# Two 64-column halves for the last key tile of the product with V, and other places for the products of a pair

## The chip, the cores and the metric

The kernel runs on one NeuronCore of a Trainium2 chip. The metric is the device time of one execution in microseconds, the median of several runs; smaller is better. Beside it there is one profiled execution, from which all durations below come.

## What is computed

Attention over 4 batches, 8 heads, 576 positions and 64 elements per head, with a bias from a small network over the distance of two positions, and behind it a mixture of experts: every token takes one of 8 experts (a local gate may keep the expert of the token before), goes through its two layers and is scaled by the gate's probability.

```python
scores = scale * np.matmul(q, k.transpose(0, 1, 3, 2))
...
scores = scores + bias.transpose(2, 0, 1)[None, :, :, :]
scores = scores - np.max(scores, axis=-1, keepdims=True)
attn = np.exp(scores)
attn = attn / (np.sum(attn, axis=-1, keepdims=True) + 1e-09)
return np.matmul(attn, v).astype(np.float32)
...
h = np.maximum(x[b, s] @ w1[e], 0.0)
out[b, s] = p[e] * (h @ w2[e])
```

## The kernel before

**Pairs and units.** Attention goes by pairs `(p, b)`: two heads x = 0, 1 of batch b, 16 pairs in all. The 576 queries of a pair are five tiles, in the order `QORD` = 1, 2, 0, 3, 4; a full tile is two units, one for each head, and the last tile, of 64 queries, is one unit for both. A pair is thus nine units, numbered u. The first four pairs (p = 0) run interleaved, while the bias is still being made; the other twelve run one after the other.

**One unit.** `emit_s` multiplies q with k in fp16 (L305, L306; L316 for the last tile) into one of two PSUM tiles `sps`. VectorE adds the bias and takes the row's extreme (L325), ScalarE takes the exponential with the row sum (L330). `emit_t` transposes the result on TensorE (L396, the last keys in L412, for the last tile L410), and ScalarE and VectorE copy it into the tile `eT` (L402, L400, L413).

**Product with V.** `emit_av(p, b, g)` multiplies `eT` with V in fp32 for a group of query tiles: g = 0 holds tiles 1 and 2 (256 columns), g = 1 tiles 0, 3 and 4 (320 columns). The output is a PSUM tile `av` with head 0 in partitions 0 to 63 and head 1 in 64 to 127; there is one such tile. Keys 512 to 575 of both heads make up a common tile j = 4, V being laid out with zeros so that a single product over 128 columns serves both (L422). For j = 0 to 3 each head has a product of 64 columns (L426). In group 1 a small product (L434) folds the two row sums of the last query tile into columns 320 and 321. VectorE copies `av` to `xt` (L440) and the sums to `sums` (L442).

For eight pairs (`DMP`, the first eight behind p = 0) group 0 goes another way: the probabilities are split into two fp16 parts (L336, L346), SP's queue transposes them by DMA (L350), and `av_split` multiplies them in three parts n = 0, 1, 2 (L363 for the last keys, L369 in 64-column halves, 8 for each part), with a copy to `xt` (L380).

Behind group 1, `emit_recip` inverts the sums, `emit_gates` multiplies `xt` with the gate weights (L534 for p = 2 and 3, into a free part of the same PSUM tile), and `emit_rows` transposes `xt` back (L454, L456), scales it (L466, L471), splits it in two fp16 parts and stores it through SP, five units later for the eight split pairs.

**The order.** Every step is entered with a key, its unit plus an offset, and the steps are issued in the order of the keys. SP's queue keeps that order from the first to the ninth pair behind p = 0; on the other engines a planner may still pass over a step that isn't ready and issue a later one. S of unit u has the key u, the DMA steps and stores u + 0.1, other steps u + 0.4, transposes u + `LTS`, the parts of `av_split` u + `LA0` (u is the last unit of tile 2), `emit_av` of group 0 u + `LAN`, and counted from the unit of the last tile, `emit_av` of group 1 u + `LA1`, gates u + `LL`, rows u + `LOUT`. The pairs with p = 0 have offsets of their own (`LB0`, `LC0`, `LO0`), which stay. Counted from the first unit of a pair, u is 3 for tile 2 and 8 for the last tile. The last pair's products stand in a part written out by hand.

Of the kernel before, what the change touches and what calls it, by code (L numbers as in the profile page):

```python
# [49 lines left out]
def build(tc, nc, io):  # L50
# [6 lines left out]
    def load_pack(name, fields):  # L57
        t = const.tile(list(io[name].shape), F32, name="c_" + name)
        nc.sync.dma_start(out=t, in_=io[name])
        views, o = [], 0  # L60
        for w in fields:
            views.append(t[:, o:o + w])
            o += w
        return views
# [38 lines left out]
    ident, wgl, c8e, s0m, tokv, c128, iota, emadd, amat, gmat, edif, fold, hmask, bcut = load_pack("cpb", CPB)  # L103
# [158 lines left out]
    e_t, eT_t, hs_t = {}, {}, {}  # L262
# [153 lines left out]
    def emit_av(p, b, g, part=None):  # L416
        n = (256, 320)[g]
        if part != 1:
            av_t[p, b] = av_ps.tile([128, 512], F32, name="av")
        av, eT, vt = av_t[p, b], eT_t[p, b, g], v_t[b, p]  # L420
        if part != 1:
            nc.tensor.matmul(out=av[:, 0:n], lhsT=vt[:, 4], rhs=eT[:, 8, 0:n], start=True, stop=False)  # L422
        js = (0, 1, 2, 3) if part is None else (0, 1) if part == 0 else (2, 3)
        for j in js:
            for x in range(2):
                nc.tensor.matmul(  # L426
                    out=av[64 * x:64 * x + 64, 0:n], lhsT=vt[:, j, 64 * x:64 * x + 64],
                    rhs=eT[:, 2 * j + x, 0:n], start=False, stop=(j == 3),
                )
        if part == 0:  # L430
            return
        eT_t.pop((p, b, g))
        if g == 1:
            nc.tensor.matmul(out=av[0:64, 320:322], lhsT=fold, rhs=hs_t.pop((p, b)), start=True, stop=True)  # L434
        if g == 0:
            xt_t[p, b] = xt_p.tile([128, SP], F32, name="xt")
            if p >= NP - 2:
                nc.vector.memset(xt_t[p, b][:, S:SP], 0.0)
        xt = xt_t[p, b]
        nc.vector.tensor_copy(out=xt[:, 256 * g:256 * g + n], in_=av[:, 0:n])  # L440
        if g == 1:
            nc.vector.tensor_copy(out=sums[0:64, p, 4, b], in_=av[0:64, 320:322])  # L442
# [107 lines left out]
    def rtile(shape, name, dt=F32):  # L550
        return rbox["p"].tile(shape, dt, name=name)
# [83 lines left out]

    bias_step(12)
    LB0, LC0, LO0 = 3.2, 6, 1.28
    LTS = (3.2, 3.2, 2.95, 3.2, 3.95)
    LA0, LAN, LA1, LL, LOUT = (5.8, 8.55, 8.8), 10.62, (6.35, 6.6), 8.6, 8.72
    NU = len(units)  # L640
    ex_t = {}

# [427 lines left out]
    def pair_av1(p, b, part):  # L1070
        emit_av(p, b, 1, part)
        if part != 0:
            emit_recip(p, b)
# [3 lines left out]
    def at(key, f, *a):  # L1077
        ev.append((key, len(ev), partial(f, *a)))

    for u in range(NU):  # L1080
        gi, hh = units[u]
        p, b, qt = groups[gi]
        at(u, unit_s, u)
        at(u + 0.1, unit_r, u)
        at(u + (LB0 if p == 0 else LTS[QORD.index(qt)]), emit_t, u)
        at(u + 0.4, unit_x, u)
        if qt == QORD[1] and hh == 1:
            if (p, b) in DMP:
                for n in range(3):
                    at(u + LA0[n], av_split, p, b, n)  # L1090
            elif p:
                at(u + LAN, emit_av, p, b, 0)
            else:
                at(u + LC0 + 0.6, emit_av, p, b, 0)
        if qt == 4:
            if p:
                if LA1[0] == LA1[1]:
                    at(u + LA1[0], pair_av1, p, b, None)
                else:
                    at(u + LA1[0], pair_av1, p, b, 0)  # L1100
                    at(u + LA1[1], pair_av1, p, b, 1)
                at(u + LL, pair_gates, p, b)
                at(u + LOUT, pair_out, (p, b, gi))
            else:
                at(u + LC0 + 0.6, pair_av1, p, b, None)
                at(u + LC0 + LO0 - 0.01, pair_gates, p, b)
                at(u + LC0 + LO0, pair_out, (p, b, gi))
# [57 lines left out]
    out = io["out"]  # L1165
# [12 lines left out]
    oa, at = rtile([128, NG2, NB], "oa", F16), rtile([128, NG2, NB], "at", F16)  # L1178
# [63 lines left out]
    with fin:  # L1242
# [16 lines left out]
        for i in range(2):  # L1259
            nc.tensor.matmul(  # L1260
                out=cn[:, i:i + 1], lhsT=amat16[:, i], rhs=R["cs"][:, S - 1:S], start=True, stop=True
            )
        nc.vector.tensor_scalar(
            out=nbc.rearrange("p a k -> p (a k)"), in0=bcut[0:32], scalar1=cn[:, 0:1], scalar2=None, op0=ALU.is_lt
# [7 lines left out]
        for i in (2, 3):  # L1272
            nc.tensor.matmul(out=cn[:, 2 + i:3 + i], lhsT=amat[:, i], rhs=nb[:, 2:3], start=True, stop=True)
        nc.vector.scalar_tensor_tensor(
            out=R["thh"], in0=nb[:, 1:2], scalar=128.0, in1=cn[:, 1:2], op0=ALU.mult, op1=ALU.subtract
        )
        nc.vector.scalar_tensor_tensor(
            out=gp[:, 1], in0=cn[:, 1:2].to_broadcast([32, B]), scalar=-1.0, in1=gmat, op0=ALU.add, op1=ALU.mult
# [5 lines left out]
            out=rbox["h16"][:, 0:S], in0=R["cs"], scalar=R["thh"], in1=es, op0=ALU.is_gt, op1=ALU.mult  # L1284
# [3 lines left out]
            out=ecm[:, K1:NF], in0=c128[0:8, 0:NF - K1], scalar1=cn[0:8, 3:4], scalar2=None, op0=ALU.is_ge  # L1288
        )
        nc.vector.tensor_scalar(  # L1290
            out=ecm[:, NF:], in0=c128[0:8, 0:NH], scalar1=cn[0:8, 5:6], scalar2=None, op0=ALU.is_ge
        )
        nc.vector.tensor_scalar(
            out=hsh, in0=cn[:, 4:5], scalar1=cn[:, 3:4], scalar2=128.0 * (NF - K1), op0=ALU.subtract, op1=ALU.add
# [10 lines left out]
            out=ez, in0=ecm.unsqueeze(2).to_broadcast([8, NBLK, NE]),  # L1305
# [14 lines left out]
        for b in range(K1, K1 + 2):  # L1320
# [4 lines left out]
            out=mkp.rearrange("p k e -> p (k e)"), lhsT=on[0:8, 0:128], rhs=ez.rearrange("p k e -> p (k e)"),  # L1325
            start=True, stop=True,
        )
        for b in range(K1, K1 + 2):
# [6 lines left out]
            out=mk, in0=mkp, in1=emadd.unsqueeze(1).to_broadcast([128, NBLK, NE]), op=ALU.add  # L1335
# [19 lines left out]
        for i, m in enumerate((FSURE, HSURE)):  # L1355
            nc.vector.tensor_scalar(
                out=rest[:, i:i + 1], in0=emp[:, NBLK + i:NBLK + i + 1], scalar1=-float(m), scalar2=0.0,
# [5 lines left out]
            out=i1, in0=sls, scalar1=0.0, scalar2=float(NT // 2 - 1), op0=ALU.is_lt, op1=ALU.add  # L1363
# [5 lines left out]
            out=odh, in0=i1[:, NF:NF + HSURE], scalar1=2.0, scalar2=hmask[:, 1:2], op0=ALU.mult, op1=ALU.add  # L1369
# [155 lines left out]
```

## Time and profile before

| | us |
|---|---|
| median of 3 runs | 581.85 |
| lowest and highest | 580.81 and 583.0 |
| profiled execution, device time | 579.53 |
| its span in the profile | 577.7 |

The span goes from the first to the last instruction of the profiled execution; the device time holds about 1.8 us more around it. Engines are named PE (TensorE's matmuls), PEld (its weight loads), DVE (VectorE), ACT (ScalarE), POOL (GpSimd) and SP (the DMA queue). A number like L426 is a line of the kernel before.

### The profile page before, as it was taken

To read this page: it belongs to the slowest core of one execution; us is meant where nothing else is said; L and a number is where in the kernel's file an instruction comes from. 1 tells how busy PE (TensorE), PEld (TensorE's weight loads), DVE (VectorE), ACT (ScalarE), POOL (GpSimd) and SP (SyncE) were. 2 spreads that over 40 slices of the span, in tenths; PEclk is the share of its full clock that TensorE was granted. 3 is DMA by queue.
4 is the path that set the end of the run, shared out by engine and by line. 5 is a ranking of instruction groups with operands and counts; after the bars stand their busy time and mean duration, and the time that the engine had idled before them with its cause. 6 is when DMAs were issued, how large, how long until landed. Compare 5 with 4: busy or idle time off the path is not lost. (4 is left out here: it accounts for less than half of the span.)

```text
span 577.7 us, 14240 instructions
## 1 busy us (share of the span) xinstructions
PE 530.2 (92%) x5302; PEld 359.0 (62%) x5319; DVE 468.2 (81%) x914; ACT 436.6 (76%) x742; POOL 260.4 (45%) x293
## 2 busy tenths in 40 slices
PE   5679999989978999999899999999999999999991
PEld 1124445756755667767586676577686867777851
DVE  6888885688888989797888468779999799898950
ACT  5879877867978887877589865468998787986840
POOL 5200000795299969858547560622433354334111
PEclk9799999999999999999999998799999999999997
DMA  8766546756798799646084012866999947878240
GB/s 278 258 175 186 143 133 194 262 161 154 193 240 226 204 255 247 188 105 190 23 289 117 2 42 71 218 220 218 290 260 293 332 146 191 161 214 225 36 180 30
DMA packets 99613, 106.15 MB, mean 184 GB/s; under 512 B 66893, under 2 KB 76239, under 8 KB 95442
## 3 DMA queue, kind: packets, MB, share of 16 engines
q1 hardware_dynamic: 94752, 89.45, 55.0%
q0 software_dynamic: 4640, 15.43, 9.1%
q8 instruction: 44, 0.72, 0.5%
q10 hardware_dynamic: 146, 0.30, 0.2%
q14 instruction: 31, 0.25, 0.1%
HBM read 128.92 MB, written 20.80 MB: 259 GB/s over the span
## 5 line engine op out<-in xcount | busy, mean ns | idle before, releaser
L330 ACT ACTIVATE e<-e,st 128x576 f32<-128x576 f32 x144 | 111.5, 776 | 16.5 <-DVE st L325 13.1
L325 DVE CUSTOM_DVE_ANT_0 e<-sps,wb 128x576 f32<-128x576 f32 x144 | 107.0, 749 | 18.1 <-PE sps L306 13.3
L917 DVE TENSOR_TENSOR w<-wb,w 128x2048 bf16<-128x2048 f32 (+1 forms) x36 | 72.3, 2050 | 1.9 <-ACT w L910 1.6
L402 ACT COPY eT<-ta 128x512 f32<-128x512 f32 x96 | 55.0, 582 | 21.8 <-PE ta L396 14.6
L305 PE MATMUL sps<-kh,qs 128*128 128x288 f16 x256 | 68.3, 288 | 3.4 <-DVE st L325 2.8
L1014 POOL DMA_INDIRECT out_dram<-y,odx x17 | 30.3, 1781 | 90.2 <-ACT y L1004 58.9
L396 PE MATMUL ta<-c_cpb,e 128*128 128x128 f32 x448 | 70.1, 277 | 0.2
L306 PE MATMUL sps<-kl,qs 128*128 128x288 f16 x256 | 68.0, 286 | 0.0
L910 ACT CAST w<-wb 128x2048 f16<-128x2048 f32 (+1 forms) x40 | 63.8, 1641 | 2.6 <-DMA wb<-in_w_dram 2.6
L988 PE MATMUL yp<-w,hhT 128*128 128x512 f16 (+1 forms) x255 | 64.3, 384 | 1.5 <-ACT w L910 0.5
L211 PE MATMUL sps<-hd,c_cpa 128*32 128x512 f32 (+17 forms) x352 | 49.2, 517 | 15.0 <-DVE hd L197 10.6
L949 PEld LDWEIGHTS <-we 128*128 128x128 f16 (+1 forms) x1056 | 59.9, 98 | 2.4
L949 PE MATMUL sps<-xT,we 128*128 128x128 f16 (+1 forms) x1056 | 61.1, 219 | 0.0
L426 PE MATMUL av<-eT,vt 128*64 128x320 f32 (+1 forms) x384 | 60.8, 424 | 0.0
L396 PEld LDWEIGHTS ta<-c_cpb,e 128*128 128x128 f32 x448 | 52.0, 141 | 10.0 <-issue 2.2
L197 DVE TENSOR_SCALAR hd<-tab,bp 128x448 f32<-128x448 f32 (+17 forms) x130 | 50.1, 445 | 3.6 <-PE sps L211 3.6
L949 PE MATMUL sps<-xT,wb 128*128 128x128 f16 (+3 forms) x1056 | 50.1, 209 | 0.7 <-issue 0.7
L949 PEld LDWEIGHTS <-wb 128*128 128x128 f16 (+1 forms) x1056 | 48.1, 99 | 3.8 <-issue 2.5
L917 DVE TENSOR_TENSOR we<-ws,we 128x2048 bf16<-128x2048 f32 (+1 forms) x25 | 48.9, 1995 | 1.1 <-ACT we L910 1.1
L988 PEld LDWEIGHTS <-hhT 128*128 128x128 f16 x272 | 26.2, 100 | 30.3 <-issue 3.0
L426 PEld LDWEIGHTS av<-eT,vt 128*64 128x64 f32 x384 | 26.2, 136 | 26.6 <-issue 10.4
L910 ACT CAST we<-ws 128x2048 f16<-128x2048 f32 (+1 forms) x26 | 41.2, 1636 | 0.0
(234 smaller groups left out, 1013.2 us busy)
## 6 DMA issues: line engine op xcount, KB each, us to landing
ws<-in_w_dram SPq DMA_DIRECT2D x34, 1024.0 KB
wb<-in_w_dram SPq DMA_DIRECT2D x34, 1024.0 KB
hs<-in_w_dram SPq DMA_DIRECT2D x20, 1024.0 KB
bias_d<-bv SPq DMA_DIRECT2D x36, 295.5 KB
kf<-in_kt_dram SPq DMA_DIRECT2D x24, 288.0 KB
wb<-bias_d SPq DMA_DIRECT2D x16, 288.0 KB
wb<-bias_d SPq DMA_DIRECT2D x16, 256.0 KB
xrow_d<-xo SPq DMA_DIRECT2D x16, 256.0 KB
```

Source lines behind the costliest of these rows:

```text
L197: nc.vector.tensor_scalar(out=hd[:, 0:n], in0=tab[:, 0:n], scalar1=bp[:, k:k + 1], scalar2=0.0, op0=ALU.add, op1=ALU.max,)
L305: nc.tensor.matmul(out=ps[:, half, 0:288], lhsT=lq, rhs=kh[:, j], start=True, stop=False)
L306: nc.tensor.matmul(out=ps[:, half, 0:288], lhsT=lq, rhs=kl[:, j], start=False, stop=True)
L325: nc.vector.tensor_tensor_reduce(out=e, in0=ps[:, :, 0:288], in1=bsl, scale=-0.125, scalar=1e30, op0=ALU.add, op1=ALU.min, accum_out=st[:, ...
L330: nc.scalar.activation(out=e, in_=e, func=AF.Exp, scale=-1.0, bias=st[:, 0:1], accum_out=sm)
L396: nc.tensor.transpose(out=ta[:, j, :], in_=e[:, o:o + 128], identity=ident)
L402: nc.scalar.copy(out=eTv[:, :, hh, o:o + 128], in_=ta)
L426: nc.tensor.matmul(out=av[64 * x:64 * x + 64, 0:n], lhsT=vt[:, j, 64 * x:64 * x + 64], rhs=eT[:, 2 * j + x, 0:n], start=False, stop=(j == 3),)
L910: nc.scalar.copy(out=wh[c][:, sl], in_=src)
L917: nc.vector.tensor_tensor(out=wl[c][:, sl], in0=src, in1=wh[c][:, sl], op=ALU.subtract)
L949: nc.tensor.matmul(out=hp.rearrange("p a j -> p (a j)")[:, n * f:n * f + n], lhsT=w[f // 4][:, o:o + 128], rhs=x[:, kt], start=(i == 0), s ...
L988: nc.tensor.matmul(out=yp, lhsT=x[:, kt], rhs=w[kt // 4][:, 512 * (kt % 4):512 * (kt % 4) + 512], start=(i == 0), stop=(i == len(terms) - 1),)
```

## The change

The last key tile's product becomes two halves of 64 columns, one for each head, in the loop with the other four key tiles, in which it is the first. The fold of the row sums is issued ahead of the products instead of behind them. `emit_av` of group 1 is issued as a whole, at one key. All offsets of transposes are 3.2, and the offsets of the parts of `av_split`, of both groups of `emit_av`, of gates and rows are others.

```diff
-        if part != 1:
-            nc.tensor.matmul(out=av[:, 0:n], lhsT=vt[:, 4], rhs=eT[:, 8, 0:n], start=True, stop=False)
-        js = (0, 1, 2, 3) if part is None else (0, 1) if part == 0 else (2, 3)
+        if part != 1 and g == 1:
+            nc.tensor.matmul(out=av[0:64, 320:322], lhsT=fold, rhs=hs_t.pop((p, b)), start=True, stop=True)
+        js = (4, 0, 1, 2, 3) if part is None else (4, 0, 1) if part == 0 else (2, 3)
         for j in js:
             for x in range(2):
                 nc.tensor.matmul(
                     out=av[64 * x:64 * x + 64, 0:n], lhsT=vt[:, j, 64 * x:64 * x + 64],
-                    rhs=eT[:, 2 * j + x, 0:n], start=False, stop=(j == 3),
+                    rhs=eT[:, 8 if j == 4 else 2 * j + x, 0:n], start=(j == 4), stop=(j == 3),
                 )
         if part == 0:
             return
         eT_t.pop((p, b, g))
-        if g == 1:
-            nc.tensor.matmul(out=av[0:64, 320:322], lhsT=fold, rhs=hs_t.pop((p, b)), start=True, stop=True)
...
-    LTS = (3.2, 3.2, 2.95, 3.2, 3.95)
-    LA0, LAN, LA1, LL, LOUT = (5.8, 8.55, 8.8), 10.62, (6.35, 6.6), 8.6, 8.72
+    LTS = (3.2, 3.2, 3.2, 3.2, 3.2)
+    LA0, LAN, LA1, LL, LOUT = (5.22, 6.22, 7.22), 7.6, 7.6, 8.24, 8.25
...
-                if LA1[0] == LA1[1]:
-                    at(u + LA1[0], pair_av1, p, b, None)
-                else:
-                    at(u + LA1[0], pair_av1, p, b, 0)
-                    at(u + LA1[1], pair_av1, p, b, 1)
+                at(u + LA1, pair_av1, p, b, None)
```

## Rows read from the trace of the kernel before

**Rows 1.** Page, table of engines: busy time, share of the span, instructions.

```profile
PE 530.2 (92%) x5302; PEld 359.0 (62%) x5319; DVE 468.2 (81%) x914; ACT 436.6 (76%) x742; POOL 260.4 (45%) x293
```

**Rows 2.** Busy time by stretch: start:end, length, engines, granted clock, DMA share, GB/s.

```profile
130.00:262.00 132.00, 123.27 (x1082) 86.88 (x1083) 114.97 (x293) 108.62 (x250) 95.85 (x107) 1.00 0.78 203
...
sum 207.00, PE 195.29 PEld 137.63 DVE 167.83 ACT 167.89 POOL 143.78; mean PE 97.65 PEld 68.81 DVE 83.91 ACT 83.94 POOL 71.89
```

**Rows 3.** TensorE's waits, 130 to 337 us: total, times, longest.

```profile
PE av L363 <- DMA eT<-e: 5.2, 3, 3.3
...
PE av L534 <- DVE sums L442: 0.7, 1, 0.7
...
PE ta L454 <- DVE sums L442: 0.6, 1, 0.6
PE av L422 <- DVE xt L380: 0.6, 2, 0.3
```

**Rows 4.** TensorE's timeline, a call of group 1: start, busy, instruction.

```profile
244.53 0.70 PE L422 MATMUL av<-eT,vt 128*128 128x320 f32 x2
245.07 0.29 PE L305 MATMUL sps<-kh,qs 128*128 128x288 f16 x1
...
246.20 2.37 PE L426 MATMUL av<-eT,vt 128*64 128x320 f32 x16
248.40 0.23 PE L434 MATMUL av<-hs,c_cpb 128*64 128x2 f32 x2
```

**Rows 5.** The same view, a call of group 0 with 256 columns.

```profile
295.91 0.60 PE L422 MATMUL av<-eT,vt 128*128 128x256 f32 x2
296.34 0.29 PE L305 MATMUL sps<-kh,qs 128*128 128x288 f16 x1
...
296.83 0.60 PE L396 MATMUL ta<-c_cpb,e 128*128 128x128 f32 x4
297.27 0.29 PE L305 MATMUL sps<-kh,qs 128*128 128x288 f16 x1
...
300.18 1.95 PE L426 MATMUL av<-eT,vt 128*64 128x256 f32 x16
302.06 0.30 PE L305 MATMUL sps<-kh,qs 128*128 128x288 f16 x1
```

**Rows 6.** The same view, a call made in pieces.

```profile
317.56 0.65 PE L426 MATMUL av<-eT,vt 128*64 128x256 f32 x4
318.14 0.66 PE L396 MATMUL ta<-c_cpb,e 128*128 128x128 f32 x4
318.73 0.65 PE L426 MATMUL av<-eT,vt 128*64 128x256 f32 x4
```

**Rows 7.** Groups by line: busy us, mean ns of one, idle before.

```profile
L426 PEld LDWEIGHTS av<-eT,vt 128*64 128x64 f32 x384 | 26.2, 136 | 26.6 <-issue 10.4 <-ACT e L330 0.9 <-ACT eT L400 0.7
...
L369 PE MATMUL av<-eT,v 128*64 128x256 f16 x192 | 13.3, 276 | 0.0
...
L422 PEld LDWEIGHTS av<-eT,vt 128*128 128x128 f32 x48 | 7.3, 191 | 1.6 <-DVE xt L380 1.2 <-DVE eT L413 0.3
```

**Rows 8.** VectorE's timeline around the copies of one pair.

```profile
218.28 1.88 DVE L346 TENSOR_TENSOR e<-e,e 128x1152 f16<-128x1152 f32 x1
220.08 0.48 DVE L440 COPY xt<-av 128x320 f32<-128x320 f32 x1
220.48 0.14 DVE L442 COPY sums<-av 64x2 f32<-64x2 f32 x1
```

**Rows 9.** TensorE's timeline, the same pair.

```profile
218.51 0.23 PE L434 MATMUL av<-hs,c_cpb 128*64 128x2 f32 x2
...
220.68 1.30 PE L534 MATMUL av<-c_cpb,xt 128*128 128x32 f32 x10 [0.66 <-DVE sums L442]
```

**Rows 10.** The same view, products of the split scheme in two pairs.

```profile
166.51 0.49 PE L363 MATMUL av<-eT,v 128*128 128x256 f16 x3 [3.26 <-DMA eT<-e]
166.93 1.50 PE L369 MATMUL av<-eT,v 128*64 128x256 f16 x24
...
241.70 1.06 PE L369 MATMUL av<-eT,v 128*64 128x256 f16 x16
242.69 0.65 PE L396 MATMUL ta<-c_cpb,e 128*128 128x128 f32 x4
```

## The prediction

> **What bounds the kernel now.** I began with the table of engines on the page: TensorE is busy for 92% of the span [rows 1], more than any other engine. An average over stages hides which wait ends last, so I next cut out the stage in which the moved steps lie, from 130 to 337 us (first pair of heads whose places change, to the last product with V). There TensorE is busy for 195.29 of 207.00 us at full granted clock [rows 2], so 11.7 us of its time are free. VectorE and ScalarE have 39 us each. In this stage the end is set by TensorE: a change pays if it takes work off TensorE or fills some of those 11.7 us, and costs if it opens new gaps.
>
> Then I asked what TensorE waits for there [rows 3]. The largest item, 5.2 us in three places, is the first product L363 of the split scheme waiting for the transposing DMA of its fp16 probabilities (3.26 us in one pair [rows 10]). Of the rest only three items touch what the diff moves: L534 and L454 waiting for VectorE's copies out of the product's PSUM tile (0.7 and 0.6 us), and L422 waiting for the tile to be emptied by L380 (0.6 us). Together 1.9 us. What is left (route steps, S matmuls waiting for VectorE) does not depend on the edited lines.
>
> Last I read TensorE's timeline in order. It shows two more things. The order on TensorE is not the written one: L422 stands at 244.53 us, S matmuls follow, and L426 of the same call comes at 246.20 [rows 4]. So keys such as `LA1` are wishes; a planner fills in by what it holds to be ready. And the products in 64-column form are broken up: two of a call's halves, transposes, two more [rows 6].
>
> **The change, part by part.**
>
> *Two halves for the last key tile.* A call of `emit_av` issues 2 matmuls at L422 now (fp32 takes two passes), 4 halves after. There are 24 such calls, so 48 instructions become 96. Price at 320 columns: L422 to the next matmul takes 245.07 - 244.53 = 0.54 us; 16 halves at L426 take 248.40 - 246.20 = 2.20 us, so 4 take 0.55 [rows 4]. At 256 columns: 296.34 - 295.91 = 0.43 us, against 16 halves in 302.06 - 300.18 = 1.88 us, so at most 0.47 for 4, with the cost of leaving the form included [rows 5]. The difference is 0 to +0.04 us per call, at most +1 us for 24; I take 0, because two halves clearly stream side by side.
>
> The weight loads double in count: 136 ns for a 64-column load against 191 ns [rows 7], so 0.54 against 0.38 us per call. They are hidden under the matmuls: 16 halves of 256 columns are 0.117 us apart, less than one load.
>
> The Trainium skill speaks against this part: "TensorE: Matmul & The Clock Gate", Part 3, says that a weight load runs under matmuls in flight only when it goes to another group of rows. Both halves use all 128 rows, so by that rule loads would stand between the matmuls. By that rule, rival four follows; the spacing below one load [rows 5, 7] does not agree with it.
>
> *What a change of form costs.* Where four halves stand alone among transposes, they take 318.14 - 317.56 = 0.58 us instead of the 0.43 of the same work in the whole form, and the four transposes behind them 318.73 - 318.14 = 0.59 instead of 297.27 - 296.83 = 0.44 [rows 5, 6]. A separate visit to the 64-column form thus costs about 0.30 us. For the fp16 products, 24 in one run are busy for 1.50 us and one lasts 0.276 [rows 7, 10], so they are (1.50 - 0.28) / 23 = 0.053 us apart; the 16 that take 242.69 - 241.70 = 0.99 us pay 0.14 for leaving. Entering costs 166.93 - 166.51 = 0.42 less three products L363 of 256 columns at 0.107, 0.10 [rows 10]; a visit 0.24. I counted visits along the timeline of the stage: the 16 calls of `emit_av` behind the first round of pairs are made in 26 visits, the 8 calls of `av_split` in 14. So 10 x 0.30 + 6 x 0.24 = 4.4 us are spent on products that do not stand together. The halves themselves add no visit when contiguous with L426, and would add one (0.30 us) wherever the planner pulls them ahead as it now does with L422 in 5 of the 16 calls: 0 to +1.5 us. I take 0, since all their operands are old by the new keys.
>
> *Parts of `av_split`.* Keys 5.8 / 8.55 / 8.8 become 5.22 / 6.22 / 7.22. Part 0 keeps its place in effect: between the two keys lies only the step function at 0.4, no S matmul and no transposes. So the 5.2 us of DMA waits stay; the transposes on SP are issued from unit steps that don't move. Parts 1 and 2 move ahead of two or one S groups, so when the data lands all 24 halves are next in turn, as already happens in three pairs. I take the 6 extra visits as gone: -1.4 us. What pays is one S group delayed by 0.86 us, with two S tiles in PSUM as cover; if VectorE has run dry, it costs up to 0.86 - 0.50 = 0.4 us in a pair. PSUM comes free earlier, so L422's 0.6 us wait should go.
>
> *Products of the second group (`LA1`), gates and output.* `emit_av` goes from units 14.35 and 14.6 of a pair to 15.6, gates from 16.6 to 16.24, output from 16.72 to 16.25. Against S groups (whole units) and transposes (3.2 behind) only `emit_av` changes place, by one S group and one group of transposes. Gates and output stay between the same S groups; their stores on SP are queued five units on, as before, for the eight split pairs, and in the last four pairs move past that unit's weight load only. Nothing waits on them there. But the gap between product and gates shrinks from two S groups and two groups of transposes to one of each: (296.83 - 296.34) + 0.44 = 0.93 us [rows 5], plus 0.15 for leaving the form, 1.08 us. In it VectorE must copy. Copy and row sums take 220.62 - 220.08 = 0.54 us; but in the worst pair they stood behind the 1.88 us subtraction L346 [rows 8], and the copies ended 2.1 us after the last product began [rows 9], so TensorE stood still for 0.66. So the bounds per pair are 0 and 2.11 - 1.08 = 1.03 us. The subtraction is due at unit 13.1, so with the product one unit later it should be over before the copies: I take the low end, and +0.5 us over the 12 pairs for chance meetings. The 1.9 us of waits I halve: -1.0. Queued behind a waiting L534 are S matmuls, and behind those VectorE.
>
> *First group of the last four pairs (`LAN`), fold, `LTS`.* The key falls from 10.62 to 7.6, so the two products of a pair no longer meet; fewer pieces there, more pieces of the later second group, which now serves as filler: 0, between -3.0 (all ten extra visits gone) and +3.0 (as many more). The fold in front takes its 0.16 us off the wait for the copy, hidden: 0. Transposes of the fifth tile come 0.75 units earlier, those of the third 0.25 later: 0, hidden by the 2-buffer tiles.
>
> Sum: 0 - 1.4 - 1.0 + 0.5 = -1.9 us. The profiled execution took 579.53 us (span 577.7, 1.8 around it) and would take 577.6; it lies 2.3 below the median of the runs, 581.85, on which I set the forecast: **580.0 us**, 0.3% less. About 0.5%, 2.9 us, is what such a measurement can tell from no change.
>
> **Rivals.**
> 1. *All stands together.* Every extra visit goes and all 1.9 us of waits too: -4.4 - 1.9 = -6.3 us, 575.6. For it: the diff joins the parts. Against: the planner breaks calls up for readiness, whatever the keys.
> 2. *The copies are caught on TensorE's path.* The 0.93 us between product and gates don't cover VectorE. If the eight split pairs all answer in 2.11 us: 8 x 1.03 - 1.3 paid now = +6.9 us, 588.8; if half do, +2.8, 584.7. It decides against the change once the 12 pairs answer in over 1.4 us on average, (2.9 + 1.3) / 12 above 1.08. For it: 0.66 us were paid even with the longer gap [rows 9]. Against: the long subtraction moves away, and the planner may slide an S group in.
> 3. *The keys do nothing.* The planner puts the products where they were: 581.9. For it: rows 4. Against: keys differ by over a unit.
> 4. *Loads stand between the halves.* Every load adds to its matmul: 4 x (0.136 + 0.1375) - 2 x (0.191 + 0.27) = +0.17 us per call, about 4.1 us for 24: 586.0. [rows 7] against rows 5.
>
> **How the numbers follow.** Forecast 47% (its own range 577.5 to 582.5, of which 8 points are below 578.9), rival 1 27%, rival 2 17%, rival 3 7%, rival 4 2%. So faster 0.27 + 0.08 = 0.35, no change 0.39 + 0.07 = 0.46, slower 0.19. The range goes below rival 1 by the unknown of the pieces and up to half of rival 2: 574.5 to 586.
>
> **What would show it.** TensorE's timeline: 4 halves before L426 in 0.43 to 0.55 us; 24 fp16 halves in one run in all eight pairs; fewer than 40 visits. Waits: L534 and L454 for VectorE below 1.3 us, none of L422's successor for L380; 5.2 us for the DMA about unchanged. I am wrong if waits for the copies exceed 3 us, if pieces grow in number, or if DMA waits move by several us because the transposing DMAs fall elsewhere.

## The result, and the profile after

| | before | after |
|---|---|---|
| median | 581.33 us (6 runs, 575.51 to 583.0) | 587.16 us (6 runs, 585.13 to 589.79) |
| ratio, 95% interval | | 1.0122, 1.0084 to 1.0159 |
| span of the profiled execution | 577.7 us | 584.8 us |

The changed kernel is 1.2% slower, above the predicted 574.5 to 586.0. Ratios here and below are worked out from the fast runs of both kernels, so they are not the quotients of the medians (1.0100 here). A number like L426 below is a line of the kernel that is spoken of; in the changed kernel L426 is all halves, L422 the fold, L452 to L454 the rows, L532 the gates.

The page's table of engines, and busy time by stretch (start:end, length, engines, granted clock, DMA share, GB/s), which answer to [rows 1, 2]:

```profile
PE 537.5 (92%) x5350; PEld 362.4 (62%) x5367; DVE 467.8 (80%) x914; ACT 437.2 (75%) x742; POOL 262.6 (45%) x293
```

```profile
130.00:262.00 132.00, 123.83 (x1061) 86.42 (x1059) 110.47 (x282) 104.86 (x241) 95.84 (x106) 0.99 0.77 198
...
sum 207.00, PE 196.00 PEld 135.52 DVE 164.30 ACT 163.24 POOL 139.52; mean PE 98.00 PEld 67.76 DVE 82.15 ACT 81.62 POOL 69.76
```

In the same 207 us TensorE is as busy as before (196.00 against 195.29), but gets through less: VectorE and ScalarE, which work on what it delivers, fall from 167.83 and 167.89 to 164.30 and 163.24 us, and 130 to 262 holds 1061 matmuls instead of 1082, though the change adds matmuls. So it is not idle time that grew but what the same work costs.

TensorE's waits from 130 to 337 us, as in [rows 3] (total, times, longest):

```profile
PE av L363 <- DMA eT<-e: 5.2, 4, 2.2
PE av L426 <- DVE eT L413: 1.2, 3, 0.5
...
PE av L422 <- DVE xt L380: 0.9, 1, 0.9
```

The waits for the copies at the gates and rows (0.7 and 0.6 us) are gone, the DMA waits unchanged in sum; the wait for L380, now in front of the fold, is 0.9 us instead of 0.6, and 1.2 us are new, halves that come up on the heels of the copy of the last key tile (L413). Nowhere does a new wait explain 6 us.

TensorE's timeline: a call of 320 columns with the fold in front, then pieces of the next pair's call, all from the changed kernel (start, busy, instruction).

```profile
267.01 0.28 PE L422 MATMUL av<-hs,c_cpb 128*64 128x2 f32 x2
267.15 0.73 PE L426 MATMUL av<-eT,vt 128*64 128x320 f32 x2
267.81 0.66 PE L396 MATMUL ta<-c_cpb,e 128*128 128x128 f32 x4
268.40 2.90 PE L426 MATMUL av<-eT,vt 128*64 128x320 f32 x18
271.24 0.30 PE L305 MATMUL sps<-kh,qs 128*128 128x288 f16 x1
...
290.14 0.76 PE L426 MATMUL av<-eT,vt 128*64 128x320 f32 x4
290.83 0.30 PE L305 MATMUL sps<-kh,qs 128*128 128x288 f16 x1
```

A half (one head, one key tile) is two rows, since fp32 takes two passes. (The prediction counted the rows: its "16 halves" are eight here.) One half standing alone at 267.15 takes 267.81 - 267.15 = 0.66 us until the next instruction can begin. Two halves, one of each head, at 290.14 take 290.83 - 290.14 = 0.69. **A half is free only if one of the other head runs beside it.** The 18 rows, nine halves, take 2.84 us, where sixteen rows took 2.20 [rows 4]: the ninth costs 0.54 and the way out the rest. So this call, cut into one half and nine, pays twice.

I call a row of 64-column products (halves and the fold, which counts also where it stands alone) with no other instruction between a *stretch*, and one with an odd number of halves *odd*; the product over 128 columns of the kernel before is no part of one. Counted in TensorE's order in the compiled program, over all 24 calls: 40 stretches, 16 odd before; 57 and 34 after. In four pairs the call of group 1 is cut behind its third half, as here:

```profile
153.52 1.29 PE L426 MATMUL av<-eT,vt 128*64 128x320 f32 x6 [0.27 <-DVE eT L413]
154.75 0.30 PE L305 MATMUL sps<-kh,qs 128*128 128x288 f16 x1
...
155.83 2.37 PE L426 MATMUL av<-eT,vt 128*64 128x320 f32 x14
```

Before, the last key tile was one product for both heads, in one piece wherever it stood; now it is two more halves between which the planner may cut.

Where TensorE's time went: I added up, from 125 us to the last transposes of rows, the time from each matmul's start to the next one's, less idle time.

| us on TensorE | before | after |
|---|---|---|
| products with V in fp32 and fold (18 calls) | 55.4 | 60.9 |
| transposes L396, L410, L412, and of rows | 55.9 | 58.2 |
| fp16 products | 15.7 | 16.7 |
| S, gates, other | 74.7 | 74.4 |
| idle | 12.5 | 11.6 |
| end of attention, us from the start | 339.35 | 346.85 |

The products are 5.5 us dearer, of 7.5 in all; the transposes rose by 2.3 us. The fp16 products' 1.0 us are clock: behind a wait of 1.64 us for the DMA the granted clock stood at 0.50 of full speed, that is at 1.2 GHz, for a while, and 24 halves took 2.77 us instead of 1.50; no transpose fell into that time. Over the whole run the clock doesn't explain the loss: its mean was 0.981 in the six runs of the changed kernel, and 0.978 to 0.979 in the runs of the kernel before that the experiments are compared with. Window and timeline:

```profile
216.00:219.40 3.40, 3.40 (x29) 2.39 (x29) 1.35 (x2) 2.84 (x7) 3.05 (x4) 0.50 0.30 112
```

```profile
215.57 0.50 PE L363 MATMUL av<-eT,v 128*128 128x256 f16 x3 [1.64 <-DMA eT<-e]
216.00 2.77 PE L369 MATMUL av<-eT,v 128*64 128x256 f16 x24
```

### The profile page after: what moved, and what is told of

The parts are those of the page before. It is cut to its first block, busy times and chain, and to the rows that moved or that the text cites. A ratio compares the mean times of both kernels' runs of the same rounds, so it can differ in the third digit from the quotient of the medians.

```text
span 584.8 us, 14333 instructions
## 1 busy us (share of the span) xinstructions
PE 537.5 (92%) x5350; PEld 362.4 (62%) x5367; DVE 467.8 (80%) x914; ACT 437.2 (75%) x742; POOL 262.6 (45%) x293
## 5 line engine op out<-in xcount | busy, mean ns | idle before, releaser
L426 PE MATMUL av<-eT,vt 128*64 128x320 f32 (+1 forms) x480 | 81.2, 424 | 1.2 <-DVE eT L413 1.2
L396 PE MATMUL ta<-c_cpb,e 128*128 128x128 f32 x448 | 70.5, 277 | 1.2 <-ACT eT L402 1.2
L211 PE MATMUL sps<-hd,c_cpa 128*32 128x512 f32 (+17 forms) x352 | 48.5, 505 | 14.9 <-DVE hd L197 10.2
L396 PEld LDWEIGHTS ta<-c_cpb,e 128*128 128x128 f32 x448 | 51.9, 141 | 13.0 <-issue 4.0
L426 PEld LDWEIGHTS av<-eT,vt 128*64 128x64 f32 x480 | 39.7, 136 | 23.4 <-issue 7.2
L947 PEld LDWEIGHTS <-wb 128*128 128x128 f16 (+1 forms) x1056 | 46.9, 98 | 2.8 <-issue 1.5
L947 PE MATMUL sps<-xT,wb 128*128 128x128 f16 (+3 forms) x1056 | 48.5, 207 | 0.0
L305 PEld LDWEIGHTS <-qs 128*128 128x128 f16 x256 | 25.0, 98 | 27.6 <-issue 21.1
```

Of the source, the lines that this page charges most:

```text
L305: nc.tensor.matmul(out=ps[:, half, 0:288], lhsT=lq, rhs=kh[:, j], start=True, stop=False)
L396: nc.tensor.transpose(out=ta[:, j, :], in_=e[:, o:o + 128], identity=ident)
L426: nc.tensor.matmul(out=av[64 * x:64 * x + 64, 0:n], lhsT=vt[:, j, 64 * x:64 * x + 64], rhs=eT[:, 8 if j == 4 else 2 * j + x, 0:n], start=( ...
L947: nc.tensor.matmul(out=hp.rearrange("p a j -> p (a j)")[:, n * f:n * f + n], lhsT=w[f // 4][:, o:o + 128], rhs=x[:, kt], start=(i == 0), s ...
```

## The experiments

Each kernel is compared with the kernel before on the same chip. The theory is *lone halves*: stretches, and above all odd ones, make the products dearer. (Its first form, in the first four runs, spoke of broken pairs, at 0.30 us for a stretch and 0.25 more for an odd one.) Rivals: *pieces* (every stretch costs 0.30, odd or even, the prediction's price) and *places* (the keys put the products where S is held up).

**1. One part of the change alone.** `halves_only` has the two halves and the fold in front with the old keys; `keys_only` the new keys with the old last tile and fold.

```diff
 halves_only, against the kernel before
-            nc.tensor.matmul(out=av[:, 0:n], lhsT=vt[:, 4], rhs=eT[:, 8, 0:n], start=True, stop=False)
+        js = (4, 0, 1, 2, 3) if part is None else (4, 0, 1) if part == 0 else (2, 3)
 keys_only, against the kernel before
-    LTS = (3.2, 3.2, 2.95, 3.2, 3.95)
-    LA0, LAN, LA1, LL, LOUT = (5.8, 8.55, 8.8), 10.62, (6.35, 6.6), 8.6, 8.72
+    LTS = (3.2, 3.2, 3.2, 3.2, 3.2)
+    LA0, LAN, LA1, LL, LOUT = (5.22, 6.22, 7.22), 7.6, 7.6, 8.24, 8.25
```

> Only the halves and the fold in front; all keys as before. Theory (broken pairs): two 64-column halves stream side by side only when they stand next to each other, and the planner, which may now cut a call at any half, cuts it more often. In the built program the 24 calls stand in 50 stretches against 40 before, 24 of them with an odd number of halves against 16. At 0.30 us for a stretch and 0.25 us for an odd one that is +5.0 us; the change as a whole (57 stretches, 34 odd) would be +9.6 by the same prices and took 5.8, so with the same share covered about +3 us: 584 to 586. Rival (places): the loss comes from where the new keys put products, copies and gates; the halves alone cost nothing, 581 to 582.

> Only the new keys; the last key tile as one product of 128 columns, fold behind. Theory (broken pairs): 44 stretches, 26 odd, two stretches of the fp16 products less: 1.2 + 2.5 - 0.5 = +3.2 us, with the covered share off about +2: 583 to 585. Rival (places): all of the loss is here, 586 to 588.

Measured: `halves_only` 581.89 us, 1.0013 (0.9984 to 1.0043); `keys_only` 580.93 us, 0.9977 (0.9948 to 1.0005). Neither part alone makes the kernel measurably slower; together they cost 1.2%. In time both miss what the theory expected (584 to 586, 583 to 585): `halves_only` stands where *places* has it, `keys_only` 5 us below that. On TensorE, though, each part has its price: the products take 57.4 and 58.5 us against 55.4, and 2.0 + 3.1 is about the 5.5 of both. So each part may have its price in time too, hidden by something else: in the profile of `keys_only` the 5.2 us of DMA waits at L363 are missing (0.2 us), and the runs of both had a higher granted clock than those of the kernel before (see "What stays open").

**2. The whole call in one piece.** The products of a call are given priority in the planner, in either kernel.

```diff
+        with tc.high_priority():
             js = (4, 0, 1, 2, 3) if part is None else (4, 0, 1) if part == 0 else (2, 3)
             for j in js:
```

> The changed kernel with the products of a call given to the planner at a high priority, which makes it issue them in one piece as soon as they are ready: 33 stretches, none odd; nothing is computed otherwise. Theory (broken pairs): the loss goes, and more: against the kernel before 7 stretches and 16 odd ones less, 3 stretches of fp16 products more, -5.4 us by full prices, some -4 with a covered share: 576 to 580. Rival (places): the products stand earlier than by the new keys, so part of the loss goes, but not below the kernel before: 582 to 587. Rival (S held up): products ahead of everything else make VectorE and ScalarE run dry: 585 and more.

> The kernel before with the same high priority on the products of a call (last key tile in one piece of 128 columns): 29 stretches, none odd. Theory (broken pairs): 11 stretches and 16 odd ones less, -7.3 us by full prices, -5 with a covered share: 575 to 578. Rival (places): no gain, 580 to 583.

Measured: `after_prio` 593.22 us, 1.0174 (1.0133 to 1.0214); `before_prio` 585.35 us, 1.0047 (1.0015 to 1.0078). The products did become cheaper, 52.0 and 52.2 us, with no odd stretch. But a call in one piece holds up S, and TensorE then runs into VectorE's row extremes; its waits in `after_prio`, 130 to 347 us:

```profile
PE sps L305 <- DVE st L325: 7.0, 10, 1.4
```

Before, this was 1.6 us. So these kernels refute "one piece is best", and cannot judge the price of a lone half.

**3. A call in the order of the heads.** The price of a half beside one of its own head.

```diff
-        for j in js:
-            for x in range(2):
+        for j, x in [(j, x) for x in range(2) for j in js]:
```

> The kernel before with the eight halves of a call in the order of the heads (four of the first head, then four of the second) in place of alternating: 41 stretches instead of 40, the same products and columns. It prices a half that has no half of the other head beside it. 'Lone halves': a call of 320 columns takes 7 slots of 0.275 us instead of 4 (+0.83 us), one of 256 columns +0.66 us: over 12 and 4 calls 12.6 us of TensorE time, about 592 us, 588 at the least. 'Pieces' and 'places': no change, 582 us.

Measured: 588.33 us, 1.0136 (1.0083 to 1.0189), the products 63.1 us instead of 55.4. Same columns, same keys, 41 stretches instead of 40. 7.6 us of TensorE become 7.9 us of time. Its timeline:

```profile
237.99 2.42 PE L426 MATMUL av<-eT,vt 128*64 128x320 f32 x16
240.20 0.23 PE L434 MATMUL av<-hs,c_cpb 128*64 128x2 f32 x2
...
306.45 2.86 PE L426 MATMUL av<-eT,vt 128*64 128x256 f32 x16
309.24 0.30 PE L305 MATMUL sps<-kh,qs 128*128 128x288 f16 x1
```

At 306.45 sixteen rows of 256 columns take 2.79 us; with alternating heads they took 1.88 [rows 5]. By the starts of the rows, the first four run one by one, the next eight in twos, the last four one by one. At 237.99 sixteen rows take 2.21 us, as before, in twos from the first on (two rows start within 0.06 us of each other). This is not the planner's work: group 1 is issued there in two parts of two key tiles each, so that its halves stand in the order of heads 0, 0, 1, 1, 0, 0, 1, 1 in the compiled program, and in the call at 306.45 they stand in the order 0, 0, 0, 0, 1, 1, 1, 1. So TensorE ran a half beside one of the other head that comes two halves later, and not beside one that comes three or four later; direct neighbours they needn't be. Eleven of the 18 calls behind 125 us come in two parts and lose nothing by the order. That is why the products rose by 7.6 and not by the 12.6 expected, which took every call as paying.

**4. Halves bound in twos, SyncE's queue moved.** The second half of a key tile is bound right behind the first. That can't stand in the region that keeps SyncE's queue in written order, so the region was put around the other steps only.

```diff
+                with ExitStack() as sk:
+                    if x and not tail:
+                        sk.enter_context(tc.issue_after(first.ins))
+                        sk.enter_context(tc.high_priority())
-                nc.tensor.matmul(
+                    first = nc.tensor.matmul(
```

> The changed kernel, with the second half of each key tile (x = 1) bound right behind the first, so that no stretch of the products holds an odd number of halves: in the program's order 0 odd stretches (34 in the changed kernel), but 63 stretches instead of 57. Theory 'lone halves': a half with no half of the other head beside it takes a full slot, 0.25 us each at 320 columns, so 34 odd stretches cost 7 to 8 us of TensorE time, and 6 more stretches cost 6 x 0.14 = 0.8 us: about 580.5 us, between 578 and 583. Rival 'pieces' (the prediction's price, 0.30 us for each stretch, odd or even): 6 x 0.30 more, about 589 us. Rival 'places' (what costs is where the keys put the products): unchanged, 587 us.

> The kernel before with the same binding of second half to first: 2 odd stretches instead of 16, 42 stretches instead of 40. 'Lone halves': 14 x 0.25 = 3.5 us of TensorE time less, 2 x 0.14 more: about 578 us if all of it reaches the end, 580 if half does. 'Pieces': 2 x 0.30 more, 582. 'Places': 581.5.

> The new keys and the fold in front, with the last key tile in one product, and the binding: 2 odd stretches instead of 26, 47 stretches instead of 44. 'Lone halves': 24 x 0.25 = 6 us of TensorE time less: about 576 us if all of it reaches the end, 578.5 if half does. 'Pieces': 582. 'Places': 581.

Measured: 608.49, 603.51 and 606.87 us (1.0455, 1.0378, 1.0405). All miss by 4%, the kernel before among them, so the cause is not the halves: the queue had changed (about a quarter of its entries stood at other places in `before_pairs`). TensorE's waits in `before_pairs`, 130 to 337 us:

```profile
PE av L363 <- DMA eT<-e: 14.9, 7, 5.7
PE sps L505 <- DVE xt L446: 11.1, 1, 11.1
```

Their times tell nothing of the halves. Of use is TensorE's own time for the products: 55.4, 53.1 and 54.4 us against 60.9, 55.4 and 58.5 without the binding. (Other than its expectation says, `keys_pairs` has the fold behind the products, as the kernel before; so has `keys_bound` below, and `halves_bound` has it in front.)

**5. The same binding, SyncE's queue in its own order.** SyncE's instructions are chained by order edges instead; the queue is then that of the unbound kernel but for a few entries.

```diff
-    with tc.manual_schedule(engines={nc.sync.engine}):
-        run(S1, S2)
+    for key, _, f in ev:
+        if S1 <= key < S2:
+            n0 = len(nc.cur_bb.bb.instructions)
+            f()
+            for i in nc.cur_bb.bb.instructions[n0:]:
+                if i.engine == nc.sync.engine:
+                    if spq:
+                        tc.add_manual_dep(i, spq[-1].name, nosync, reason="issue_after")
+                    spq.append(i)
```

> The changed kernel with the second half (x = 1) of each key tile bound right behind the first, and this time SyncE's queue left in the changed kernel's own order (the runs with the binding so far had moved it, and TensorE waited 11 to 15 us for DMAs). In the program's order 0 odd stretches of halves instead of 34, 52 stretches instead of 57. 'Lone halves': at 0.17 us (what TensorE's time for the products fell by, per odd stretch, in the three runs with the moved queue) to 0.25 us each, 34 of them and 5 x 0.14 us: 6.5 to 9 us of TensorE time less; about 580 us, 577 to 583. 'Pieces' (0.30 us a stretch, odd or even): 5 x 0.30 = 1.5 us less, 585.5. 'Places' (the new keys cost by where they put the products): 587 us.

> The kernel before with the same binding and SyncE's queue in its own order: 2 odd stretches instead of 16, 41 stretches instead of 40. 'Lone halves': 14 x 0.17 to 0.25 = 2.4 to 3.5 us of TensorE time less: 578 to 580 us. 'Pieces' and 'places': 581.5.

> New keys and the fold in front, the last key tile in one product, with the binding and SyncE's queue in its own order: 2 odd stretches instead of 26, 43 instead of 44. 'Lone halves': 24 x 0.17 to 0.25 = 4 to 6 us of TensorE time less: 575 to 578.5 us. 'Pieces' and 'places': 581. Against after_bound this is also the price of the two halves where nothing is cut apart: 'lone halves' has the two within 1.5 us, save for 9 more stretches there (1.3 us).

> The kernel before with the last key tile as two halves (old keys, the fold at its old place), with the binding and SyncE's queue in its own order: 0 odd stretches instead of 24, 47 instead of 50. 'Lone halves': 24 x 0.17 to 0.25 + 3 x 0.14 = 4.5 to 6.4 us of TensorE time less: 576 to 579 us. 'Pieces': 581. 'Places': 582.

Measured:

| | us | ratio, 95% interval | ratio without binding |
|---|---|---|---|
| `after_bound` | 585.59 | 1.0042, 1.0000 to 1.0084 | 1.0122 |
| `before_bound` | 579.24 | 0.9956, 0.9927 to 0.9986 | 1 |
| `keys_bound` | 581.71 | 0.9984, 0.9953 to 1.0015 | 0.9977 |
| `halves_bound` | 581.67 | 0.9991, 0.9965 to 1.0017 | 1.0013 |

Binding takes 0.8% from the changed kernel (1.0042 / 1.0122 = 0.992, about ±0.006 from both intervals), two thirds of what it had lost, and 0.4% from the kernel before, whose bound form beats both kernels. `before_bound` lies in its expected range, `after_bound` above its 577 to 583. (The twelve runs of `after_bound` stand in two groups, section 6, and a median can fall into either: 585.59 against 581.32 us of the kernel before would be 0.7% slower.) *Places* is out for that part. A call of `after_bound` at the same place as the one above:

```profile
268.22 0.22 PE L424 MATMUL av<-hs,c_cpb 128*64 128x2 f32 x1
268.23 0.48 PE L432 MATMUL av<-eT,vt 128*64 128x320 f32 x1
...
268.36 0.73 PE L432 MATMUL av<-eT,vt 128*64 128x320 f32 x3
269.02 0.66 PE L396 MATMUL ta<-c_cpb,e 128*128 128x128 f32 x4
269.61 2.37 PE L432 MATMUL av<-eT,vt 128*64 128x320 f32 x16
271.91 0.30 PE L305 MATMUL sps<-kh,qs 128*128 128x288 f16 x1
```

Fold and first piece take 269.02 - 268.22 = 0.80 us as before the binding (267.81 - 267.01), but hold two halves now (1 + 3 rows); the rest takes 2.30 us instead of 2.84. One cut, at a place where it costs 0.54 us less.

`keys_bound` and `halves_bound` got cheaper products too (53.9 and 53.6 us), but no measurable time, against the 4 to 6.4 us expected. TensorE's gain there did not reach the end; idle time rose in `keys_bound` from 10.2 to 13.9 us, in `halves_bound` from 12.2 to 13.7. In the profile of `before_bound` neither: from the same S matmul near 126 us to the last transposes of rows it takes 213.3 us against 213.0, with 2.2 us less for products and 2.3 more idle. In the changed kernel it does: 217.5 us with the binding, 221.0 without.

**6. What is left in after_bound.** Its twelve runs stand in two groups, 579.03 to 581.42 us at a mean granted clock of 0.979 to 0.985, and 585.47 to 589.24 at 0.971 to 0.977. Its profiled execution is one of the second (586.7 us) and has long DMA waits, 130 to 337 us:

```profile
PE av L363 <- DMA eT<-e: 8.1, 5, 2.9
```

The suspicion: the new keys bring the fp16 products up before their data. In the three kernels the keys of `av_split` alone are moved back, or one unit on.

```diff
 after_bound_late, after_late
-    LA0, LAN, LA1, LL, LOUT = (5.22, 6.22, 7.22), 7.6, 7.6, 8.24, 8.25
+    LA0, LAN, LA1, LL, LOUT = (5.8, 8.55, 8.8), 7.6, 7.6, 8.24, 8.25
 after_bound_late1
+    LA0, LAN, LA1, LL, LOUT = (6.22, 7.22, 8.22), 7.6, 7.6, 8.24, 8.25
```

> after_bound (the changed kernel, no half alone) with one part of the key change undone: the fp16 products of a pair at their old keys 5.8, 8.55, 8.8 in place of 5.22, 6.22, 7.22. after_bound's runs fell into two groups, 579 to 581.5 us and 585.5 to 589 us, the second with the lower granted clock (0.971 to 0.978 against 0.979 to 0.985). Theory 'waits for the DMA': the new keys bring TensorE to the fp16 products before their transposing DMA has landed (8.1 us of waits in its profile), and stretches at half clock follow; with the old keys the upper group goes: about 580.5 us, mean clock of the runs 0.980 or more. Rival 'other keys' (the rest of after_bound's loss is in the tail or in the transposes): 585 us. Rival 'the split in two groups is not from these waits': two groups as before.

> after_bound with the three parts of the fp16 products one unit later (keys 6.22, 7.22, 8.22), still one part behind another. 'Waits for the DMA': 580 to 581 us, at most one wait over 1 us for the DMA in the profile. 'Other keys': 585 us. If it stays in two groups, the waits at these products do not decide it.

> The changed kernel with the fp16 products at their old keys 5.8, 8.55, 8.8 and nothing else undone: 32 odd stretches instead of 34, 58 stretches instead of 57. 'Lone halves' alone: 587 us less 2 x 0.25 us, so 586.5. 'Waits for the DMA' on top of it: it has the same lone halves, but loses the half clock that follows the waits (1.3 to 1.7 us in the changed kernel's profile): 584.5 to 585.5. If the lone halves were not what costs and the keys of the fp16 products were: 581.

Measured: `after_bound_late` 584.49 us, 1.0077 (1.0039 to 1.0115); `after_bound_late1` 582.2 us, 1.0009 (0.9972 to 1.0046); `after_late` 588.94 us, 1.0144 (1.0097 to 1.0192). The suspicion falls: later keys leave 7.1 and 7.8 us of DMA waits (6.2 in `after_late`), the runs still spread over 8 to 10 us with the clock, and undoing these keys in the changed kernel brought nothing. What they do give is a second pair for the binding, both from the same chip: 1.0077 / 1.0144 = 0.993, also about ±0.006, with the products at 54.2 instead of 60.5 us.

**All kernels together.** Stretches and odd stretches in the 18 calls behind 125 us, the same calls as in the account of TensorE's time:

| kernel | stretches | odd | products, us | by the fit |
|---|---|---|---|---|
| before | 28 | 10 | 55.4 | 55.4 |
| after | 42 | 26 | 60.9 | 60.9 |
| halves_only | 35 | 16 | 57.4 | 57.6 |
| keys_only | 32 | 20 | 58.5 | 58.3 |
| before_prio | 22 | 0 | 52.2 | 52.2 |
| after_prio | 27 | 0 | 52.0 | 52.8 |
| before_bound | 29 | 0 | 53.2 | 53.0 |
| after_bound | 40 | 0 | 54.2 | 54.3 |
| keys_bound | 31 | 0 | 53.9 | 53.3 |
| after_late | 43 | 24 | 60.5 | 60.5 |
| after_pairs | 51 | 0 | 55.4 | 55.5 |

A least-squares fit over these and five more (`halves_bound`, the two bound late ones, `before_pairs`, `keys_pairs`; all but `before_heads_apart`) gives 49.75 us + 0.113 for each stretch + 0.246 for each odd one, with 0.3 us of scatter (root mean square). With stretches alone the scatter is 2.3 us. 0.25 us is also what the timelines say: a half beside another costs 2.20 / 8 = 0.275, alone 0.54, at 320 columns. For the change: 14 x 0.113 + 16 x 0.246 = 5.5 us, what the account shows.

## Why the prediction was wrong

**The step that failed: "the halves themselves add no visit when contiguous", with the pieces of the other calls taken at 0.** The products came in more pieces, 40 to 57 over all 24 calls (26 to 38 behind the first round of pairs; with the 14 and 13 of the fp16 products 40 and 51, where fewer than 40 were to be seen). The prediction had named this sign ("if pieces grow in number") and the bounds +1.5 and +3.0 us for it, and took 0 for both: for the first because the operands are old by the new keys, for the second as the middle of -3.0 and +3.0. The products with V rose by 5.5 us. The keys don't bind: products are used as filler by the planner wherever it holds their operands to be ready, and the new form gives it two more places to cut. From `keys_only` to the changed kernel the halves add 10 stretches and 6 odd ones, 2.4 us of products; from the kernel before to `keys_only` the keys add 4 and 10, 3.1 us.

**What was mis-sized: a visit.** 0.30 us was right for the visit that it was read from, an even one [rows 6]: 0.11 in the products, the rest with the instruction behind them (the transposes of the changed kernel rose by 2.3 us on 14 more stretches, 0.16 each if all of it is put down to them). Missing was the price of an odd one, 0.25 more. The prediction read that "two halves clearly stream side by side" and did not ask when they do not; rows in odd numbers of halves were there to be read.

**What held.** The price of the two halves where nothing cuts them. An uncut call of the changed kernel:

```profile
337.71 2.38 PE L426 MATMUL av<-eT,vt 128*64 128x256 f32 x20
340.02 0.66 PE L396 MATMUL ta<-c_cpb,e 128*128 128x128 f32 x4
```

Its 20 rows take 340.02 - 337.71 = 2.31 us, as much as the product over 128 columns and the 16 rows took before, 0.43 + 1.88 [rows 5]. So rival 4 falls too: all the added loads are in these 2.31 us. The DMA waits stayed at 5.2 us. Of the 1.9 us of waits for copies the two at gates and rows vanished (1.3 us), while the one for L380, which was to go, rose to 0.9; together 1.0 us less, as taken. Rival 2, which set the slower side, has nothing in the trace. Rivals 1 and 3 fall with the count of pieces.

**"Parts of `av_split`".** Four of eight pairs have their 24 halves in one run (three before), not eight; 13 visits instead of 14. The -1.4 us did not come; one visit less is -0.24 by the prediction's price.

**What stays open.** The price on TensorE adds up; the time follows it in `before_heads_apart`, which passes its 7.6 us on in full, and in the changed kernel with its 5.5, but seems not to in `keys_only` (3.1 us without loss) and in the bound kernels. For the single parts the granted clock on record goes far. The twelve runs of `keys_only` had 0.985 in the mean and those of `halves_only` 0.981, the kernel before on the same chip 0.978. A clock higher by 0.001 went with 0.4 us less time between runs of one program (238 runs of the experiments), and 0.001 of 581 us is 0.6 us. By this estimate the clock gave `keys_only` 2.7 to 3.9 us and `halves_only` 1.3 to 1.9, about what their products had cost them (3.1 and 2.0). `before_bound` had 0.982 against 0.979, worth 1.1 to 1.6 us of its 2.6, so how much of its 0.4% is the binding's stays open. Why the clock was higher no run separated. DMA waits that come and go between kernels (0.2 to 9 us, from one execution each) are a candidate, but not alone: `before_bound`, the fastest of all, has 8.2 us of them. `keys_bound` is 4.6 us cheaper in products than `keys_only` and 3.7 us more idle, and why it waits instead wasn't looked into. Nor is it settled whether `after_bound`'s remaining 0.4% (0 to 0.8) is real; its two siblings stand at 1.0077 and 1.0009.

## What to carry to other kernels

When a product is divided into halves that stream side by side, price it by what may stand between them, not by the uncut call: half a couple costs as much as the whole one, and a planner will cut wherever operands allow. Bind the couple, not the whole call: an order edge on each second half took 0.7 to 0.8% off the changed kernel and 0.4% off the kernel before (part of that may be clock), while priority for whole calls cost 0.5% there and more in the changed one. And check that an experiment moves only what it names; here the first binding moved a DMA queue and cost 4%.

## What the runs showed of the hardware

- Halves of 64 columns run two at a time only with one of the other head, whose output goes to the other 64 partitions: 0.275 us each in twos, 0.54 alone (320 columns, two passes). The partner needn't be the direct neighbour: in the order of heads 0, 0, 1, 1 sixteen rows take 2.21 us, alternating 2.20. It may not be far either: with four halves of one head in a row, half of the rows run alone, 2.79 us instead of 1.88 (256 columns).
- Entering and leaving the 64-column form costs 0.113 us for each stretch in the products alone. The Trainium skill says in "TensorEngine Tiling (Array Packing)", Tiling Modes, that a change of mode drains TensorE; the fit agrees in kind and adds the number.
- Twelve runs of one program (`after_bound`) differed by 10 us, with a correlation of -0.91 between time and mean granted clock. Three of these kernels (`after_bound`, `halves_only`, `after_prio`) show the same picture in their profiles as the changed one above: a wait for the DMA, then a few us at half clock. Not every such wait does it: behind 3.26 us in the kernel before [rows 2, 10] and 2.88 us in `before_bound` the clock stayed at full, and in `keys_bound` half clock came behind 1.67 us of waiting for VectorE.
